# The largest magnitude of v, spread over the partitions by a diagonal matmul on TensorE instead of by an operation on GpSimd

## The chip, the cores and the metric

The kernel runs on one core of a Trainium2 chip. The metric is the device time of one execution in microseconds (us), as the median of several; lower is better. The core has five engines with a queue of instructions each, worked off in order: TensorE (PE in the profile; PEld is its loading of weights), VectorE (DVE), ScalarE (ACT), GpSimd (POOL) and SyncE (SP), which here issues the transfers.

## The reference

Attention with a threshold for 8 batches of 8 heads, 576 positions and 64 columns, then a gated two-layer network over all 4608 tokens:

```python
scores = scale * np.matmul(q, k.transpose(0, 1, 3, 2))
thresh = np.max(scores, axis=-1, keepdims=True) - tau
scores = np.where(scores >= thresh, scores, -1000000000.0)
scores = scores - np.max(scores, axis=-1, keepdims=True)
attn = np.exp(scores)
attn = attn / (np.sum(attn, axis=-1, keepdims=True) + 1e-09)
attn_out = np.matmul(attn, v)
# x: the heads side by side, 4608 x 512; w_in 512 x 2048, w_out 2048 x 512
h = x @ w_in
out = (h * (1.0 / (1.0 + np.exp(-h)))) @ w_out
```

Inputs of attention are float32; the weights come as float64 and are decoded on the chip.

## The kernel before

**Numbers in two halves.** Nearly all products are made with 16-bit operands that are split in a rounded part and the rest (hi and lo), three matmuls for one product. To split v, w_in and w_out into float16 they are first scaled by a power of two that belongs to the largest magnitude. For v this is done anew for each batch: `vmax` (L233) takes the largest magnitude of the four head pairs on each partition, and `vscale` calls `pow2_scales`, which reduces these four (`v_one`, L110), makes the largest over all 128 partitions known to every partition (`v_all`, L113), clamps it (`v_cl`, L116) and takes the two powers of two from its exponent (L120 to L131). `split_v` (L270 on ACT, L271 on DVE) then makes `v16`, hi and lo, which the product with the weights of attention reads. `pow2_scales` is also called for w_in and w_out, but with bounds that are already the same on all partitions, so without the step across them.

**Tiles.** Attention goes by visits of a pair of heads, and in a visit by tiles of 128 queries: batch 0 in two rounds of visits, batches 1 to 7 with nine tiles in each of four visits, 300 slots in all. A tile's work: scores on PE (L406) in one of two PSUM tiles; the maximum on DVE (L416); the exponential on ACT (L426) into one of four buffers `w`; the threshold and the sum on DVE (L435), a reciprocal (L443), the scaling on ACT (L448); then POOL rounds the weights to float16 and makes the rest (`hl`, L459, L462, L465) in one of three buffers, and a transposing DMA puts them into `wT`. Three tiles behind a visit's last, PE multiplies with v (L490), and ACT and DVE split the result to `x16` (L508, L509). POOL also makes the low half of k (`klo`, L320) and, early on, helps to decode the weights (L173, L199).

**Experts.** When all four pairs of a range of tokens are there, its 32 units are put in a list: 16 of `h` (12 matmuls each, L524, then a tanh on ACT, L532, and DVE, L533 and L547, into the buffers g, `gbuf`) and 16 quarters of `o` (12 matmuls each, L562). They are interleaved with the tiles of the next ranges at a rate that spreads them. After the last tile only units are left.

**PSUM.** Unit outputs take banks in turn, by `bank`: two while the weights' sums are taken, three later. A turn is given out in the order of the program's text; the instruction that writes the bank has to wait for the readers of the bank's tenant before.

**Order.** The program is written slot by slot (a slot is a tile), and each step has its slot: `vmax` of pair p of batch b 34 - 9p slots before the batch's first slot u, `vscale` at u - 2, `split_v` at u + 9p + 4, and for batch 0 at slots 0, 1 and 26. A scheduler then orders each engine's queue by readiness on its own timeline, with priorities, so that steps with nothing to wait for come well before their slot. What depends on a buffer or a bank stays behind the step that frees it.

Of the kernel before, what the change touches and what calls it, by code (L numbers as in the profile page):

```python
# [10 lines left out]
BF16 = mybir.dt.bfloat16  # L11
# [8 lines left out]
P = 128  # L20
# [8 lines left out]
GB = 17  # buffers of g: a group of 16 and one ahead  # L29
WSPARE = 2  # raw weights lie this far ahead of the split ones, which take their place  # L30
LOAD = 5  # tiles that the loads of q and k run ahead
AV_LAG = 3  # tiles from a visit's last to its product with v
EARLY = 36  # tiles in which ACT still rounds the weights of attention for GpSimd
GAP, GAP1 = 12, 1  # free slots before batch 0's second visits and before batch 1
V_SLOT = 26  # batch 0's values are split from here on
RATES = (1.3, 0.8)  # units of the experts per slot while batch 0's two groups are there
RATE = 0.95
# weights: first chunk, slots of the decoding and of the splitting, priority
# [3 lines left out]
# a visit of two heads: its tiles of 128 queries (4: the last 64 of both heads) for the  # L42
# first and the second head, and the query ranges that it completes
# [8 lines left out]
def attention_moe(  # L52
# [21 lines left out]
    # three banks in turn; the last one is for the sums of the weights while they come in  # L74
# [7 lines left out]
    # ---------------------------------------------------------------- constants  # L82
    tau_sb = const.tile([P, 1], F32, name="tau_sb")
    nc.sync.dma_start(out=tau_sb, in_=tau)
    # 1/8 where the threshold can be met (tau >= 0), else 0: all scores equal, all kept
# [9 lines left out]
    # stacks of (hi; lo) rows of q, with 64 zero columns for the shared tile  # L95
# [9 lines left out]
    def pow2_scales(mx, name, across=True):  # L105
        """From mx [P, n] (bounds >= 0, per partition or, without across, the same on all):
        s = 2^(13-e) and 1/s for the largest's exponent e."""
# [3 lines left out]
        if across:  # L111
            allp = const.tile([P, 1], F32, name=f"{name}_all", tag=f"{k}_all")
            nc.gpsimd.partition_all_reduce(allp, one, P, bass.bass_isa.ReduceOp.max)  # L113
            one = allp
# [21 lines left out]
    # ---------------------------------------------------------------- weights  # L136
# [29 lines left out]
    def decode_weights(i):  # L166
        """float64 words to float32: the sign, 8 bits of the exponent (2^-112 on the top word
        read as float32 takes the exponent's bias down), 23 of the fraction."""
# [15 lines left out]
        # sums of the magnitudes over the rows of four chunks, four columns at a time: they  # L184
        # bound h (w_in), w_out
# [33 lines left out]
    # ---------------------------------------------------------------- values  # L219
# [56 lines left out]
    # ---------------------------------------------------------------- q and k  # L276
# [12 lines left out]
    def qcol(h, i):  # L289
        """Column of query tile i in the stack (even: 0..3, last, zeros; odd: zeros, last,  # L290
        2, 3, 0, 1)."""
        return i * P if h % 2 == 0 else (0, 384, 512, 128, 256)[(i + 1) % 5]
# [30 lines left out]
    # the first visits work in float32 throughout: the tensor engine has time for them  # L323
# [53 lines left out]
    # ---------------------------------------------------------------- scores  # L377
    # a tile: (visit, [(head, query tile, first row, rows)])
# [98 lines left out]
    # ---------------------------------------------------------------- attn @ v  # L477
    x16 = {}

    def av(v, p, c0, n):  # L480
        """w @ v of the pair's two heads, side by side in the columns of the array: (w hi + w lo) @
        v hi + w hi @ v lo."""
        b = visits[v][0]
        vt = v16[b, p]
# [296 lines left out]
```

## Time and profile before

| | |
|---|---|
| timed runs, median of 3 | 1358.73 us (1357.87 to 1359.26) |
| profiled execution, first to last instruction | 1360.4 us |
| PE busy | 1183.7 us, 87% |
| DVE busy | 1002.8 us, 74% |
| ACT busy | 817.5 us, 60% |
| POOL busy | 789.9 us, 58% |
| mean granted clock of TensorE | 0.95 |

The profile is of one execution beside the timed ones; its span is the only time of it that is shown, 1.7 us above their median. A busy share is a mean over the whole span; the profile also gives it in 40 slices and in any stretch that is asked for. A row of a timeline reads: start, duration, engine, line, operation, output and inputs with their shapes, and in brackets how long the engine was idle before it and what released it; "issue" there means that nothing in the profile released it. A row of stretches gives for each engine the busy time and, in parentheses, the number of instructions, then the granted clock, the share of the DMA engines and GB/s.

### The profile page before, as it was taken

How to read it: one execution, taken by the hardware profiler on the slowest of the kernel's cores; microseconds unless marked ns; L12 is line 12 of the kernel's file. 1: busy time of each engine (PE TensorE's matmuls, PEld its weight loads, DVE VectorE, ACT ScalarE, POOL GpSimd, SP SyncE). 2: the span in 40 equal slices, each digit the busy share in tenths (PEclk: the TensorE clock that was granted, in tenths of full speed). 3: DMA queues.
4: the chain of work that ended last, by engine and by line, in shares of the span. 5: the costliest groups of instructions: out<-in, count | busy, mean ns of one | idle time of the engine just before them, and what ended most of it. 6: DMA issues, size and time to landing. Idle time of an engine off the chain costs nothing.

```text
span 1360.4 us, 26858 instructions
## 1 busy us (share of the span) xinstructions
PE 1183.7 (87%) x9392; PEld 899.9 (66%) x9392; DVE 1002.8 (74%) x2619; ACT 817.5 (60%) x1493; POOL 789.9 (58%) x964
## 2 busy tenths in 40 slices
PE   3774787898599979898899969899799999999998
PEld 2453555666477757676677757677577777777777
DVE  4987997897598967968497856869478787872421
ACT  3776775675476756656375745757367666662432
POOL 2647984787478656754476646556467666661000
PEclk9887888999799999999899979999799999999999
DMA  6454955778467656664475556565466565543000
GB/s 226 140 185 125 197 129 94 146 139 170 88 133 155 122 106 129 131 128 86 99 132 124 118 96 136 101 127 121 82 122 116 115 129 115 106 88 53 6 19 18
DMA packets 363479, 158.15 MB, mean 116 GB/s; under 512 B 329552, under 2 KB 338256, under 8 KB 363344
## 3 DMA queue, kind: packets, MB, share of 16 engines
q1 hardware_dynamic: 363344, 156.43, 55.5%
q8 instruction: 74, 1.21, 0.4%
q14 instruction: 61, 0.50, 0.1%
HBM read 66.72 MB, written 9.44 MB: 56 GB/s over the span
## 4 chain that ended last, share of the span: by engine, by line
DVE 35%; PE 34%; issue 13%; ACT 6%; POOL 6%; DMA 5%; SPq 2%; POOLq 0%; ACTq 0%; DVEq 0%
PE o L562 15%; PE h L524 8%; DVE w L435 8%; DVE sm L416 6%; DVE gbuf L547 6%; PE s L406 5%; PE a L490 5%; DVE qstack L310 3%; DVE th L533 3%; DMA vraw<-in_vL 2%; DMA wT<-hl 2%; ACT w L426 2%; POOL hl L459 2%; POOL hl L462 2%; ACT w L448 2%
## 5 line engine op out<-in xcount | busy, mean ns | idle before, releaser
L524 PE MATMUL h<-x,wst 128*128 128x288 f16 (+2 forms) x3072 | 422.3, 290 | 22.6 <-DVE th L533 19.1
L562 PE MATMUL o<-gbuf,wst 128*128 128x288 f16 (+2 forms) x3072 | 419.4, 293 | 22.4 <-DVE gbuf L547 16.1
L562 PEld LDWEIGHTS <-wst 128*128 128x128 f16 x3072 | 296.4, 100 | 117.1 <-issue 27.1
L459 POOL TENSOR_SCALAR hl<-w 128x576 f16<-128x576 f32 x264 | 187.3, 710 | 317.9 <-ACT w L448 69.1
L524 PEld LDWEIGHTS <-wst 128*128 128x128 f16 x3072 | 290.7, 99 | 119.2 <-issue 37.5
L462 POOL TENSOR_TENSOR hl<-w,hl 128x512 f16<-128x512 f32 x272 | 332.0, 1220 | 28.0 <-issue 13.9
L426 ACT ACTIVATE w<-s,sm 128x576 f32<-128x576 f32 x288 | 211.0, 736 | 204.5 <-POOL hl L465 135.4
L435 DVE SCALAR_TENSOR_TENSOR w<-s,sm,w 128x576 f32<-128x576 f32 x288 | 232.6, 810 | 110.4 <-ACT w L426 108.7
L448 ACT ACTIVATE w<-w,sm 128x576 f32<-128x576 f32 x288 | 218.2, 770 | 86.5 <-DVE sm L443 81.6
L416 DVE TENSOR_REDUCE sm<-s 128x1 f32<-128x576 f32 x288 | 215.1, 748 | 44.4 <-PE s L406 42.3
L406 PE MATMUL s<-khi,qstack 128*128 128x288 f32 x608 | 160.4, 346 | 70.0 <-DVE w L435 36.9
L547 DVE SCALAR_TENSOR_TENSOR gbuf<-th,gbuf 128x288 f16<-128x288 f32 (+2 forms) x256 | 167.3, 656 | 20.9 <-ACT gbuf L541 20.2
L406 PEld LDWEIGHTS s<-khi,qstack 128*128 128x128 f32 x608 | 98.5, 198 | 98.8 <-issue 71.4
L490 PE MATMUL a<-wT,v 128*64 128x288 f16 (+1 forms) x1680 | 142.4, 294 | 16.1 <-DMA wT<-hl 15.0
L532 ACT ACTIVATE th<-h,msc 128x288 f32<-128x288 f32 (+2 forms) x256 | 126.3, 495 | 49.5 <-DVE gbuf L547 30.0
L541 ACT ACTIVATE gbuf<-th 128x288 f16<-128x288 f32 (+2 forms) x252 | 109.9, 438 | 44.5 <-DVE th L533 43.9
L406 PE MATMUL s<-klo,qstack 128*128 128x288 f32 x608 | 134.2, 304 | 0.0
L533 DVE SCALAR_TENSOR_TENSOR th<-th,h 128x288 f32<-128x288 f32 (+2 forms) x256 | 113.2, 444 | 27.6 <-ACT th L532 25.4
L490 PEld LDWEIGHTS <-v 128*64 128x64 f16 x1680 | 91.3, 110 | 56.7 <-issue 41.9
L465 POOL TENSOR_TENSOR hl<-w,hl 128x64 f16<-128x64 f32 x272 | 115.3, 424 | 0.0
L406 PEld LDWEIGHTS s<-klo,qstack 128*128 128x128 f32 x608 | 102.2, 197 | 0.0
L320 POOL TENSOR_TENSOR klo<-kraw,khi 128x576 fp32r<-128x576 f32 x64 | 95.6, 1493 | 1.4 <-ACT khi L318 1.3
(82 smaller groups left out, 868.8 us busy)
## 6 DMA issues: line engine op xcount, KB each, us to landing
qraw<-in_qT SPq DMA_DIRECT2D x128, 144.0 KB, 3.0
kraw<-in_kT SPq DMA_DIRECT2D x128, 144.0 KB, 3.0
vraw<-in_vL SPq DMA_DIRECT2D x32, 320.0 KB, 3.5
wraw<-in_w_out SPq DMA_DIRECT2D x16, 512.0 KB, 4.0
out_t<-ot SPq DMA_DIRECT2D x56, 144.0 KB, 2.0
wT<-hl SPq DMA_TRANSPOSE x304, 3.3
gbuf<-in_w_in SPq DMA_DIRECT2D x8, 512.0 KB, 5.1
wraw<-in_w_in SPq DMA_DIRECT2D x8, 512.0 KB, 4.9
```

What stands on the lines that cost most here:

```text
L406: nc.tensor.matmul(s_ps[:, j, :HALF], lhs, kk[:, j * HALF : (j + 1) * HALF], start=(n == 0), stop=(n == len(seq) - 1),)
L416: nc.vector.tensor_reduce(out=negm, in_=s_ps[:, :, :HALF], op=ALU.max, axis=AX.XY, negate=True)
L426: nc.scalar.activation(wtile[t].rearrange("p (j c) -> p j c", j=2), sps[t][:, :, :HALF], AF.Exp, bias=small[t][:, 0:1],)
L435: nc.vector.scalar_tensor_tensor(out=w3, in0=s_ps[:, :, :HALF], scalar=sm[:, 1:2], in1=w3, op0=ALU.is_ge, op1=ALU.mult, accum_out=sm[:, 2:3],)
L448: nc.scalar.activation(w, w, AF.Copy, scale=r)
L459: nc.gpsimd.tensor_scalar(out=fl[:, 0:S], in0=w, scalar1=1.0, scalar2=1.0, op0=ALU.mult, op1=ALU.mult)
L462: nc.gpsimd.tensor_tensor(out=fl[:, 640:1152], in0=w[:, 0:512], in1=fl[:, 0:512], op=ALU.subtract)
L490: nc.tensor.matmul(a_ps[odd * D : (odd + 1) * D, :n], vt[:, lo_v, odd, kv, :], wT[v, b * H + 2 * p + odd][:, kw, c0 - base : c0 - base + n ...
L524: nc.tensor.matmul(ph[:, :n], wi(c, f, lo_w), x16[b, lo_x][:, c, c0 : c0 + n], start=(k == 0), stop=(k == 11),)
L533: nc.vector.scalar_tensor_tensor(out=th[:, :n], in0=th[:, :n], scalar=1.0, in1=ph[:, :n], op0=ALU.add, op1=ALU.mult,)
L547: nc.vector.scalar_tensor_tensor(out=g[:, 1, :n], in0=th[:, :n], scalar=2.0**-14, in1=g[:, 0, :n], op0=ALU.mult, op1=ALU.subtract,)
L562: nc.tensor.matmul(ps[:, :n], wo(f, d, lo_w), g[:, lo_g, :n], start=(f == 0 and k == 0), stop=(f == NF - 1 and k == 2),)
```

## The change

In `pow2_scales` the branch `across` is replaced. ACT multiplies the rows of an identity matrix (float32, there since the start) with the partition's own largest magnitude, which gives a diagonal matrix in bfloat16. One matmul with a matrix of ones puts the whole diagonal onto every partition, in a PSUM bank taken by `bank`. A DVE reduction takes the maximum over those 128 values. The bfloat16 rounding can move a value up to the next power of two, no further. Nothing else of the code differs but the comments, which are gone in the changed file; its lines from there on have numbers higher by five.

```diff
         if across:
-            allp = const.tile([P, 1], F32, name=f"{name}_all", tag=f"{k}_all")
-            nc.gpsimd.partition_all_reduce(allp, one, P, bass.bass_isa.ReduceOp.max)
-            one = allp
+            diag = const.tile([P, P], BF16, name=f"{name}_diag", tag="diag")
+            nc.scalar.activation(diag, ident, AF.Copy, scale=one)
+            allp = bank([P, P], f"{name}_ps")
+            nc.tensor.matmul(allp, ones, diag, start=True, stop=True)
+            one = const.tile([P, 1], F32, name=f"{name}_all", tag=f"{k}_all")
+            nc.vector.tensor_reduce(out=one, in_=allp, op=ALU.max, axis=AX.X)
```

The scheduler moves much with it. The numbers behind the names below are those of the buffers, and differ between the two programs for the same tile; the number after `w_` is the tile's.

The queue of POOL at tiles 82 to 84, where batch 3's reduction stood before; "ISA" rows without operands are calls that carry no work on a tile:

```order
L459 TENSOR_SCALAR hl_3649<-w_83_3586 128x576
L113 ISA
L113 ISA v_all<-v_one 128x1
L462 ISA
L462 TENSOR_TENSOR hl_3649<-w_83_3586,hl_3649 128x512
L465 TENSOR_TENSOR hl_3649<-w_83_3586,hl_3649 128x64
```

The same place of the change:

```order
L464 TENSOR_SCALAR hl_3661<-w_83_3594 128x576
L464 TENSOR_SCALAR hl_3698<-w_84_3651 128x576
L467 TENSOR_TENSOR hl_3661<-w_83_3594,hl_3661 128x512
L470 TENSOR_TENSOR hl_3661<-w_83_3594,hl_3661 128x64
L467 TENSOR_TENSOR hl_3698<-w_84_3651,hl_3698 128x512
```

The three calls are gone, and the first halves of tiles 83 and 84 come one behind the other.

The queue of DVE at the same tiles, with the reduction on each partition and the clamping, before:

```order
L110 TENSOR_REDUCE v_one<-vmx_3760 128x1
L251 TENSOR_TENSOR msc_5630<-v_sc,i_w_sc 128x1
L252 TENSOR_SCALAR msc_5630<-msc_5630 128x1
L261 SCALAR_TENSOR_TENSOR msc_5630<-msc_5630,o_w_sc 128x1
L416 TENSOR_REDUCE sm_3675<-s_3642 128x1
L435 SCALAR_TENSOR_TENSOR w_84_3639,sm_3638<-s_3589,sm_3638,w_84_3639 128x576
L116 TENSOR_SCALAR v_cl<-v_all 128x1
L419 TENSOR_SCALAR sm_3675<-sm_3675,ntau 128x1
```

In the change `v_one` stands at the same tile, but what follows from it stands 299 rows further down, at tile 125:

```order
L315 SCALAR_TENSOR_TENSOR qstack_85<-qraw_26_5989,gate,qstack_85 64x576
L119 TENSOR_REDUCE v_all<-v_ps 128x1
L424 TENSOR_SCALAR sm_6013<-sm_6013,ntau 128x1
L440 SCALAR_TENSOR_TENSOR w_125_5974,sm_5973<-s_5895,sm_5973,w_125_5974 128x576
L121 TENSOR_SCALAR v_cl<-v_all 128x1
```

Before, the clamping followed `v_one` by six rows, and batch 3's first split of v came 122 rows behind it; now the split comes 14 rows behind `v_all`.

The queue of PE in the change, there and at batch 1 (`v_ps` is the bank with the spread diagonal, `o` and `h` are the experts' banks):

```order
L411 MATMUL s_5977<-klo_5780,qstack_87 128x288 x2
L567 LDWEIGHTS wst
L567 MATMUL o_288_0_5579<-gbuf,wst 128x288
...
L117 LDWEIGHTS ones
L117 MATMUL v_ps<-v_diag,ones 128x128
L567 LDWEIGHTS wst
L567 MATMUL o_288_0_5579<-gbuf,wst 128x288
```

```order
L117 LDWEIGHTS ones
L117 MATMUL v_ps<-v_diag,ones 128x128
L529 LDWEIGHTS wst
L529 MATMUL h_256_1_2375<-x_0_1_452,wst 128x320
L529 LDWEIGHTS wst
L529 MATMUL h_256_1_2375<-x_0_0_451,wst 128x320
L411 MATMUL s_2505<-khi_2412,qstack_85 128x288 x2
L411 MATMUL s_2505<-klo_2414,qstack_85 128x288 x2
```

The matmul is new in PE's queue, between the quarters of an expert's output; six matmuls stand between the scores and it at batch 3, and 216 expert matmuls between it and that batch's first product with v. At batch 1 that number is 26.

## The prediction

> **What bounds the kernel now.** I read the page's busy shares first, then the slices, then the instructions of the line that goes away, then one of its eight places engine by engine, and last the table by stretches.
>
> ```profile
> PE 1183.7 (87%) x9392; PEld 899.9 (66%) x9392; DVE 1002.8 (74%) x2619; ACT 817.5 (60%) x1493; POOL 789.9 (58%) x964
> PE   3774787898599979898899969899799999999998
> ```
>
> The first row says TensorE, 87% busy, and GpSimd (POOL) far from full. The slices (34 us each) say something else: from the middle on TensorE is at 9, with single dips that return about every 155 us, once per batch. So the question is what stops it there.
>
> ```profile
> L113 POOLq MODIFY_POOL_CONFIG  x16: 4/9/13, 11.6 to 951.7; - x16
> L113 POOL PARTITION_ALL_REDUCE v_all<-v_one x8: 377/378/379, 19.1 to 957.3; - x8
>   issue: 43.9, 7
>   DVE v_cl L116: 35.3, 8
> ```
>
> The all-reduce over the partitions is listed with 378 ns, eight times, 3 us in all. But POOL stood idle 43.9 us ahead of seven of them with nothing to wait for, and VectorE (DVE) waited 35.3 us for the eight results. Here is the one of batch 5, by the timelines of POOL, DVE, ACT and PE:
>
> ```profile
> 637.34 0.67 POOL L459 TENSOR_SCALAR hl<-w 128x576 f16<-128x576 f32 x1
> 643.85 0.38 POOL L113 PARTITION_ALL_REDUCE v_all<-v_one  x1 [5.84 <-issue]
> 651.19 0.67 POOL L459 TENSOR_SCALAR hl<-w 128x576 f16<-128x576 f32 x1 [6.96 <-issue]
> ...
> 644.26 0.15 DVE L116 TENSOR_SCALAR v_cl<-v_all 128x1 f32<-128x1 f32 x1 [5.78 <-POOL v_all L113]
> 653.29 0.74 ACT L426 ACTIVATE w<-s,sm 128x576 f32<-128x576 f32 x1 [13.28 <-POOL hl L465]
> 646.05 3.16 PE L562 MATMUL o<-gbuf,wst 128*128 128x288 f16 x13 [4.90 <-DVE gbuf L547]
> 655.04 0.82 PE L406 MATMUL s<-khi,qstack 128*128 128x288 f32 x2 [4.55 <-DVE sm L443]
> ```
>
> POOL stands for 5.84 + 0.38 + 6.96 = 13.2 us, the second gap being in front of an ordinary instruction. Two stalls of TensorE follow. First DVE holds its in-order queue at `v_cl`, behind it the last step of g (L547), for which PE waits 4.90 us. Then ACT's next exponential needs a softmax buffer that POOL has not read yet (13.28 us), DVE waits for ACT, and PE 4.55 us for DVE.
>
> In a sentence of its own: the Trainium skill ("GPSIMD Engine Reference", Instruction dispatch) has the first call of a freshly loaded GpSimd routine pay a load of about 6 us that no instruction shows. The gap in front agrees; the equal one behind is not in that rule, and by one load each POOL would stand 8 x 6 = 48 us where the trace shows 13 us each.
>
> What it costs, by stretches (us and instructions of PE, PEld, DVE, ACT, POOL, then the granted clock):
>
> ```profile
> 20.00:40.00 20.00, 9.90 (x33) 6.82 (x34) 15.06 (x32) 11.07 (x21) 10.31 (x11) 0.71 0.38 114
> 40.00:100.00 60.00, 46.24 (x270) 30.12 (x270) 55.53 (x144) 46.36 (x90) 34.77 (x33) 0.90 0.54 168
> 100.00:120.00 20.00, 9.19 (x57) 6.11 (x54) 11.80 (x31) 9.27 (x16) 10.24 (x11) 0.76 0.37 98
> 120.00:200.00 80.00, 57.88 (x397) 41.77 (x395) 79.32 (x175) 59.26 (x107) 72.87 (x75) 0.83 0.73 165
> 220.00:240.00 20.00, 15.83 (x107) 12.55 (x108) 9.93 (x33) 7.78 (x12) 12.38 (x18) 0.83 0.59 104
> 240.00:340.00 100.00, 89.09 (x703) 65.25 (x700) 85.20 (x224) 67.53 (x117) 76.05 (x94) 0.98 0.77 150
> 340.00:360.00 20.00, 8.24 (x48) 7.14 (x49) 6.35 (x26) 5.62 (x9) 7.45 (x12) 0.57 0.35 58
> 360.00:480.00 120.00, 108.34 (x896) 83.07 (x896) 112.39 (x287) 87.00 (x160) 90.27 (x109) 0.99 0.71 136
> 480.00:500.00 20.00, 15.92 (x110) 11.98 (x109) 11.39 (x37) 8.82 (x16) 6.74 (x11) 0.91 0.27 55
> 500.00:640.00 140.00, 130.94 (x1097) 100.95 (x1098) 112.37 (x299) 91.75 (x170) 89.81 (x114) 1.00 0.65 129
> 640.00:660.00 20.00, 10.55 (x52) 7.24 (x50) 8.22 (x29) 4.06 (x8) 8.19 (x12) 0.74 0.30 65
> 660.00:790.00 130.00, 125.81 (x1072) 97.96 (x1071) 104.89 (x275) 86.22 (x159) 83.74 (x104) 1.00 0.62 124
> 790.00:815.00 25.00, 13.90 (x89) 10.42 (x89) 11.09 (x36) 8.18 (x14) 10.74 (x15) 0.73 0.38 65
> 815.00:950.00 135.00, 126.80 (x1072) 97.83 (x1070) 107.26 (x281) 86.71 (x161) 81.77 (x104) 1.00 0.61 122
> 950.00:975.00 25.00, 15.73 (x89) 11.27 (x88) 10.25 (x38) 8.80 (x14) 11.32 (x17) 0.73 0.46 80
> 975.00:1240.00 265.00, 261.75 (x2221) 202.54 (x2219) 206.95 (x552) 171.34 (x318) 170.21 (x214) 1.00 0.58 110
> 1240.00:1360.00 120.00, 116.62 (x976) 92.66 (x973) 29.86 (x66) 36.59 (x78) 0.00 (x0) 1.00 0.06 18
> ```
>
> The short stretches hold the reduces of batches 1 to 7 (batch 0's is at 19 us), the long ones lie between. From 360 us on the long ones run at 0.99 to 1.00 of the clock with PE 90 to 99% busy; the short ones lose both time and clock. Before 240 us DVE is the full engine (93 and 99%), and its holes are what counts.
>
> **The change, part by part.** *Removed, batches 3 to 7.* In a short stretch I count the matmuls and divide by the rate of the long stretch behind it; the rest of the time is lost. 340: 48 matmuls at 896/120 = 7.47 per us are 6.4 us, lost 13.6. 480: 110 at 7.84, lost 6.0. 640: 52 at 8.25, lost 13.7. 790: 89 at 7.94, lost 13.8. 950: 89 at 8.38, lost 14.4. Sum 61.5 us. Idle time of PE alone is 45.7 us there; the other 16 are matmuls at the lower clock, which goes with the stall. Both come back if POOL keeps working, since PE has a full queue in the long stretches and runs 120 us of pure experts at the end: 1240 to 1360 holds 976 matmuls, 0.123 us each, that only wait for their turn.
>
> By the Trainium skill ("TensorE: Matmul & The Clock Gate", The HAM clock gate) the clock halves after an idle window of about 3.4 us; the trace agrees (0.57 to 0.91 in the stretches where PE stood 4 us and longer at a time, 0.98 and more between). Stalls that stay shorter would cost themselves alone; the sum doesn't change by it.
>
> *Removed, batches 0 to 2.* Here I count DVE's holes against its share in the next long stretch. Batch 2, 220 to 240: 0.85 x 20 - 9.93 = 7 us. Batch 1, 100 to 120: 0.99 x 20 - 11.80 = 8 us. Batch 0:
>
> ```profile
> 19.49 0.15 DVE L116 TENSOR_SCALAR v_cl<-v_all 128x1 f32<-128x1 f32 x1 [6.98 <-POOL v_all L113]
> ```
>
> 6.98 us, and 0.93 x 20 - 15.06 = 3.5 from 20 to 40 us, while POOL cannot decode weights; I take 8 of the 10.5, since the first loads are still landing. Sum 23 us; the ends are 8 (half of DVE's holes are filled by other waits, the first 8 don't shift) and 26.
>
> *Added.* Per batch one ACT copy of 128x128, one weight load and matmul of 128x128, one DVE reduction from PSUM. The nearest rows:
>
> ```profile
> L362 ACT ACTIVATE wT<-tl 128x128 f32<-128x128 f32 x16 | 4.4, 277 | 0.0
> L196 DVE TENSOR_REDUCE wmx<-wps x8: 273/280/291, 46.2 to 178.6; 128x1 f32<-128x128 f32 x8
> L191 PE MATMUL wps<-wst,ones 128*128 128x128 bf16 x128 | 13.9, 244 | 10.8 <-DVE wst L180 10.5 <-DVE sm L439 0.3
> ```
>
> 0.28, 0.28 and 0.24 us. ACT and DVE have 10% or more to spare from 360 us on; PE pays 8 x 0.24 = 2 us.
>
> *Moved.* The order shows that the matmul takes a PSUM bank in turn, so it comes when the program's text comes to it, some 30 tiles after `v_one` and the diagonal copy. PE therefore finds the diagonal ready, and no wait for ACT is added; the matmul stands 2 to 19 expert matmuls behind the scores that DVE reads just before, so DVE waits 0.2 to 2.3 us for it, inside its spare time. But the scale now lies 14 rows ahead of the first split of v. From batch 3 on PE has 216 expert matmuls, 216 x 0.123 = 27 us, between the diagonal matmul and the first product with v, ample. In batch 1 it has 26 matmuls (3.2 us) and three groups of scores, against some 18 DVE rows and two splits; I take 3 us of wait there, between 0 and the longest stall of PE that the trace has:
>
> ```profile
> 115.58 0.85 PE L406 MATMUL s<-khi,qstack 128*128 128x288 f32 x2 [10.57 <-DVE w L435]
> ```
>
> *Sum.* Against the profiled span, 1360.4 - 61.5 - 23 + 2 + 3 = 1281 us. The median of the timed runs is 1.7 us under that span, so **1279 us** is the forecast.
>
> **Rivals.** (1) *Only the first half of each stall goes.* The gap behind the reduce carries the name of no instruction; were it something else (a buffer, a transfer), only DVE's direct wait would vanish. In batch 5 that is 4.90 of the 9.45 us that PE idled, 52%; 0.52 x 84.5 = 44 us gained, and with the 5 us added 1320 us. Against it are the first ordinary POOL instructions behind the reduces of batches 3 and 7, which have the same gap, with nothing to wait for, while the page's releasers elsewhere are named:
>
> ```profile
> 349.07 1.14 POOL L462 TENSOR_TENSOR hl<-w,hl 128x512 f16<-128x512 f32 x1 [6.78 <-issue]
> ...
> 964.73 0.67 POOL L459 TENSOR_SCALAR hl<-w 128x576 f16<-128x576 f32 x1 [7.03 <-issue]
> ```
>
> (2) *The early gain doesn't arrive.* Until 240 us the order of decoding, splitting and scores is changed most, and DVE's holes there may be filled by loads; without the 23 us it is 1302 us. For it: the transfers are 0.38 to 0.73 busy there. Against: DVE's 93 and 99% just after the holes.
>
> (3) *Slower.* The late scale makes the split of v late, and the product with v, in PE's in-order queue, holds the experts behind it. It decides from the point where the chain from the diagonal matmul over DVE's reduction and six small steps to the two splits outlasts the 27 us by 84.5/8 = 10.6 us, which happens to be the longest stall above. At 13.2 us per batch, POOL's standstill put on PE, the sum is 1360.4 - 84.5 + 8 x 13.2 - 1.7 = 1380 us. Against it: the steps behind the matmul are those of `v_cl`, 0.15 us each.
>
> (4) *The reduce stays*, or the queues fall into an order that loses as much elsewhere: no change. POOL's rows hold no such instruction any more.
>
> **How the numbers follow.** Forecast 0.72; (1) 0.10; (2) 0.08; (3) 0.04; (4) 0.02; and 0.04 that yet more goes, below 1262, because the idle time in the stretches from 240 to 480 (10.9 + 11.7 us) is partly the aftermath of the stalls. The range is 1262 (three quarters of those 22.6 us gone as well) to 1312 (no early gain, and 1 us of new waiting per batch on top): it leaves out (1), (3), (4) and the lower tail, 0.20. A change of 0.2% (2.7 us) is what the measurement can tell. Faster 0.94, same 0.02, slower 0.04.
>
> **What would show it.** Right: no instruction of that line on POOL and no 6 us gaps in its queue; the granted clock at 0.98 or more in every 20 us stretch from about 300 us on; PE's busy time a little lower than 1183.7 us and its idle time near 110 us instead of 1360.4 - 1183.7 = 177; the end of attention (1240 us before) some 80 us earlier, and the pure experts behind it still about 120 us. Wrong: dips that stay once per batch, now in front of the products with v (rival 3) or of the scores with POOL as the cause (rival 1); or a start whose first 240 us are as long as before (rival 2).

## The result, and the profile after

The changed kernel takes **1283.62 us** (median of 4 runs, 1280.87 to 1284.8) against 1358.99 us for the kernel before (median of 4, 1357.87 to 1360.19). The ratio is **0.9433, 95% interval 0.9413 to 0.9453**: 75 us or 5.7% faster. The forecast was 1279 us in a range from 1262 to 1312. On another chip the same program took 1281.1 us beside 1362.58, ratio 0.9394 (0.9369 to 0.942). Among the runs below, one execution of chain_twice (2916.86 us) and one of the kernel before (2337.64 us) took about twice as long, for a reason the record doesn't show; the ratios are taken without them.

The page of the changed kernel, busy times first, then two of its rows of slices (32 us each here):

```profile
span 1282.6 us, 26842 instructions
PE 1164.2 (91%) x9400; PEld 891.7 (70%) x9400; DVE 1001.3 (78%) x2627; ACT 819.3 (64%) x1501; POOL 794.6 (62%) x956
PE   5675778799699989999999999999899999999998
PEclk8987899899999989999999999999999999999999
```

The work of DVE, ACT and POOL is what it was, within 5 us each. PE is busy 19.5 us less (1183.7 before) with eight matmuls more, so the same matmuls ran at a higher clock, and it is idle 1282.6 - 1164.2 = 118 us instead of 177. The dips once per batch are gone from the second half of the row PE, but for one 8.

The table by stretches (us and instructions of PE, PEld, DVE, ACT, POOL, then the clock, the DMA share and GB/s). The short stretches up to 760 us lie about where batches 3 to 6 now come by the step (their `v_one` is at 315, 470, 616 and 758 us, 15 to 33 us earlier than before):

```profile
100.00:160.00 60.00, 41.71 (x291) 30.55 (x292) 59.64 (x124) 43.27 (x81) 54.64 (x58) 0.83 0.71 171
160.00:200.00 40.00, 28.59 (x210) 19.28 (x209) 38.98 (x89) 26.98 (x44) 30.20 (x32) 0.96 0.61 113
...
300.00:320.00 20.00, 17.84 (x144) 13.35 (x143) 14.86 (x37) 11.37 (x19) 12.56 (x16) 1.00 0.78 164
...
455.00:475.00 20.00, 15.67 (x131) 12.46 (x130) 15.96 (x41) 9.99 (x16) 12.54 (x15) 0.94 0.56 141
475.00:600.00 125.00, 121.16 (x1008) 93.54 (x1007) 101.02 (x269) 83.28 (x156) 82.40 (x102) 0.98 0.63 122
600.00:620.00 20.00, 18.06 (x152) 14.19 (x150) 16.66 (x48) 10.26 (x17) 12.76 (x15) 1.00 0.65 148
620.00:740.00 120.00, 117.29 (x993) 90.87 (x992) 96.71 (x268) 82.04 (x154) 78.62 (x98) 1.00 0.61 121
740.00:760.00 20.00, 18.79 (x160) 14.68 (x158) 15.26 (x41) 11.00 (x19) 15.59 (x18) 1.00 0.71 161
...
1027.00:1165.00 138.00, 136.16 (x1165) 106.19 (x1163) 104.55 (x283) 87.47 (x161) 87.68 (x110) 1.00 0.56 104
1165.00:1282.00 117.00, 114.23 (x956) 90.74 (x954) 30.01 (x66) 36.37 (x77) 0.00 (x0) 1.00 0.05 16
```

At batch 5's step 152 matmuls now run in 20 us, where the stand's 20 us had 52, and at batch 6's 160; the clock is 1.00 in both. The start is still DVE's (99 and 97% busy from 100 to 200 us), and the pure experts at the end still take 117 us, behind an attention that ends 75 us sooner.

The groups of the chain that was added, with the mean of one in ns and the idle time before it:

```profile
L115 ACT ACTIVATE v_diag<-ident,v_one 128x128 bf16<-128x128 f32 x8 | 3.2, 395 | 0.0
L119 DVE TENSOR_REDUCE v_all<-v_ps 128x1 f32<-128x128 f32 x8 | 2.2, 281 | 0.0
L117 PE MATMUL v_ps<-v_diag,ones 128*128 128x128 bf16 x8 | 1.8, 220 | 0.0
```

None of the three made its engine wait. And of the waits of ACT, this one has halved; the first row is from the kernel before, the second from the changed one (us in total, times, the longest):

```profile
ACT w L426 <- POOL hl L465: 135.4, 54, 14.4
```

```profile
ACT w L431 <- POOL hl L470: 74.8, 47, 5.6
```

The next table places the gains in time, by when the n-th of the 6144 expert matmuls starts. Its head has the times of the kernel before for the 768th, 1536th, 2304th, 3072nd, 3840th and last. The stands of batches 3 and 4 lie between the first two of these times, those of batches 5, 6 and 7 one each in the next three gaps. The rows are the us by which a kernel is ahead (behind, with a minus). Each is one execution: diag_again is the changed kernel once more, and differs from it by up to 7 us; that of pool_spread was the longest of its six. The experiments follow below.

| kernel | 333 | 523 | 681 | 835 | 995 | 1356 |
|---|---|---|---|---|---|---|
| changed | 18.0 | 36.9 | 52.0 | 64.9 | 78.6 | 77.4 |
| diag_again | 18.9 | 43.4 | 57.5 | 70.4 | 85.7 | 84.6 |
| early_only | 21.6 | 18.5 | 18.2 | 18.2 | 21.7 | 14.4 |
| late_only | -2.6 | 20.2 | 35.6 | 48.0 | 62.2 | 60.6 |
| idle_reduce | -7.5 | 2.7 | 1.3 | 2.2 | 8.5 | 7.8 |
| idle_pair | -10.5 | -7.2 | -6.6 | -15.4 | -19.5 | -26.5 |
| pool_spread | 11.7 | 20.1 | 32.0 | 35.3 | 40.9 | 35.3 |
| tile_spread | 20.6 | 38.2 | 49.9 | 53.8 | 63.7 | 53.0 |
| piece_late | 19.1 | 33.9 | 45.1 | 53.6 | 63.0 | 53.9 |

The changed kernel gains 18 us up to 333 us, 19 us over the stands of batches 3 and 4 together, 13 to 15 us over each of the next three, and nothing behind.

### The profile page after: what moved, and what is told of

It is laid out like the page before. It is cut to its first block, busy times and chain, and to the rows that moved or that the text cites. A ratio compares the mean times of both kernels' runs of the same rounds, so it can differ in the third digit from the quotient of the medians.

```text
span 1282.6 us, 26842 instructions
## 1 busy us (share of the span) xinstructions
PE 1164.2 (91%) x9400; PEld 891.7 (70%) x9400; DVE 1001.3 (78%) x2627; ACT 819.3 (64%) x1501; POOL 794.6 (62%) x956
## 4 chain that ended last, share of the span: by engine, by line
PE 45%; DVE 26%; issue 8%; POOL 8%; DMA 7%; ACT 5%; SPq 1%; POOLq 0%; ACTq 0%; DVEq 0%
PE o L567 18%; PE h L529 14%; PE s L411 7%; PE a L495 6%; DVE w L440 5%; DVE sm L421 4%; DVE gbuf L552 4%; DMA wT<-hl 3%; POOL hl L467 3%; DVE qstack L315 2%; DMA vraw<-in_vL 2%; POOL hl L464 2%; DVE th L538 2%; POOL hl L470 2%; DVE wst L185 1%
## 5 line engine op out<-in xcount | busy, mean ns | idle before, releaser
L529 PE MATMUL h<-x,wst 128*128 128x288 f16 (+2 forms) x3072 | 417.2, 289 | 18.0 <-DVE th L538 16.3
L567 PE MATMUL o<-gbuf,wst 128*128 128x288 f16 (+2 forms) x3072 | 403.2, 287 | 8.2 <-DVE wst L211 5.8
L529 PEld LDWEIGHTS <-wst 128*128 128x128 f16 x3072 | 290.5, 99 | 111.8 <-issue 31.2
L567 PEld LDWEIGHTS <-wst 128*128 128x128 f16 x3072 | 289.5, 98 | 95.4 <-DVE wst L211 9.2
L467 POOL TENSOR_TENSOR hl<-w,hl 128x512 f16<-128x512 f32 x272 | 338.3, 1244 | 12.4
L552 DVE SCALAR_TENSOR_TENSOR gbuf<-th,gbuf 128x288 f16<-128x288 f32 (+2 forms) x256 | 158.6, 622 | 22.8 <-ACT gbuf L546 22.0
L495 PE MATMUL a<-wT,v 128*64 128x288 f16 (+1 forms) x1680 | 147.9, 302 | 8.4 <-DMA wT<-hl 6.8
L495 PEld LDWEIGHTS <-v 128*64 128x64 f16 x1680 | 94.7, 114 | 50.2 <-issue 39.5
L470 POOL TENSOR_TENSOR hl<-w,hl 128x64 f16<-128x64 f32 x272 | 122.0, 449 | 0.0
```

What stands on the lines that cost most here:

```text
L467: nc.gpsimd.tensor_tensor(out=fl[:, 640:1152], in0=w[:, 0:512], in1=fl[:, 0:512], op=ALU.subtract)
L470: nc.gpsimd.tensor_tensor(out=fl[:, 576:640], in0=w[:, 512:576], in1=fl[:, 512:576], op=ALU.subtract)
L495: nc.tensor.matmul(a_ps[odd * D : (odd + 1) * D, :n], vt[:, lo_v, odd, kv, :], wT[v, b * H + 2 * p + odd][:, kw, c0 - base : c0 - base + n ...
L529: nc.tensor.matmul(ph[:, :n], wi(c, f, lo_w), x16[b, lo_x][:, c, c0 : c0 + n], start=(k == 0), stop=(k == 11),)
L552: nc.vector.scalar_tensor_tensor(out=g[:, 1, :n], in0=th[:, :n], scalar=2.0**-14, in1=g[:, 0, :n], op0=ALU.mult, op1=ALU.subtract,)
L567: nc.tensor.matmul(ps[:, :n], wo(f, d, lo_w), g[:, lo_g, :n], start=(f == 0 and k == 0), stop=(f == NF - 1 and k == 2),)
```

## The experiments

All diffs are against the changed kernel; ratios are to the kernel before, on the same chip. The theory: GpSimd stands still for 13.2 us per reduction, and that, not DVE's wait for the result, is what TensorE lost.

### The reduction kept, with nobody waiting for it (idle_reduce)

```diff
         if across:
+            unused = const.tile([P, 1], F32, name=f"{name}_un", tag=f"{k}_un")
+            nc.gpsimd.partition_all_reduce(unused, one, P, bass.bass_isa.ReduceOp.max)
             diag = const.tile([P, P], BF16, name=f"{name}_diag", tag="diag")
```

> The diagonal matmul everywhere, and beside it GpSimd's all-reduce as before, into a tile that nobody reads; no engine waits for its result. Theory (POOL stands for 13 us at each, 6 in front and 7 behind, and this alone stops the softmax, while DVE's direct wait is the other half): half of the gain is lost, 1283.6 + 36 = 1320 us (1303 to 1335), PE idle in front of scores but no longer in front of the experts' second half. Rival 1 (the gap behind the reduction belongs to something else, only DVE's direct wait costs): no change from 1283.6 us (1280 to 1290). Rival 2 (DVE's direct wait was covered, POOL alone costs): 1350 us or more.

Measured: 1354.2 us, ratio 0.996 (0.9938 to 0.9981). With DVE free of its wait, 72 to 77 us of the gain are gone (0.996 against 0.9433 and 0.9394). The half that was expected to remain did not; the time is that of the second rival, 1350 us or more. Its timeline at batches 4 and 5:

```profile
513.44 0.38 POOL L115 PARTITION_ALL_REDUCE v_un<-v_one  x1 [6.02 <-issue]
520.87 0.67 POOL L466 TENSOR_SCALAR hl<-w 128x576 f16<-128x576 f32 x1 [7.05 <-issue]
523.08 0.74 ACT L433 ACTIVATE w<-s,sm 128x576 f32<-128x576 f32 x1 [7.09 <-POOL hl L472]
524.83 0.51 PE L413 MATMUL s<-khi,qstack 128*128 128x288 f32 x2 [2.45 <-DVE w L442]
...
662.31 0.38 POOL L115 PARTITION_ALL_REDUCE v_un<-v_one  x1 [6.31 <-issue]
669.62 1.14 POOL L469 TENSOR_TENSOR hl<-w,hl 128x512 f16<-128x512 f32 x1 [6.93 <-issue]
671.06 0.74 ACT L433 ACTIVATE w<-s,sm 128x576 f32<-128x576 f32 x1 [10.70 <-POOL hl L472]
672.81 0.82 PE L413 MATMUL s<-khi,qstack 128*128 128x288 f32 x2 [9.60 <-DVE w L442]
```

In batch 5 PE waits 9.60 us in one go, where it had waited 4.90 and 4.55. The first wait is gone, and the second is as long as the two were together, which fits one cause for both, POOL at a stand. Batch 4 shows the other side: there the stand met a moment at which ACT lost only 7.09 us, and PE then waits 2.45.

### Two such reductions (idle_pair)

```diff
+            unused = const.tile([P, 1], F32, name=f"{name}_un", tag=f"{k}_un")
+            nc.gpsimd.partition_all_reduce(unused, one, P, bass.bass_isa.ReduceOp.max)
+            unused = const.tile([P, 1], F32, name=f"{name}_uo", tag=f"{k}_uo")
+            nc.gpsimd.partition_all_reduce(unused, one, P, bass.bass_isa.ReduceOp.max)
```

> As the run with the unread all-reduce, with two of them per batch. In batches 0 to 4 they stand back to back in POOL's queue, in batches 5 to 7 the scheduler puts one tile's three rounding instructions between them. Theory (the gaps are GpSimd exchanging its code, paid when the kind of instruction changes): back to back the second costs 0.4 to 0.8 us more and POOL stands 13.6 to 14 us; where they are apart each has its own gaps, two times 13 us; the whole is 10 to 35 us slower than with one. Rival (the gaps are the reduction's own time, which the 378 ns don't show): POOL stands 19 to 26 us at a pair back to back too, and the whole is 30 to 60 us slower than with one.

Measured: 1387.82 us, ratio 1.0211 (1.0164 to 1.0257), 33.6 us above the single one. POOL's timeline in batch 4, where the two stand back to back, and in batch 5, where ordinary instructions came between them:

```profile
514.30 0.38 POOL L115 PARTITION_ALL_REDUCE v_un<-v_one  x1 [5.83 <-issue]
514.60 0.42 POOL L117 PARTITION_ALL_REDUCE v_uo<-v_one  x1
522.24 1.14 POOL L471 TENSOR_TENSOR hl<-w,hl 128x512 f16<-128x512 f32 x1 [7.22 <-issue]
...
670.24 0.38 POOL L115 PARTITION_ALL_REDUCE v_un<-v_one  x1 [5.87 <-issue]
677.70 1.14 POOL L471 TENSOR_TENSOR hl<-w,hl 128x512 f16<-128x512 f32 x1 [7.09 <-issue]
...
685.14 0.38 POOL L117 PARTITION_ALL_REDUCE v_uo<-v_one  x1 [6.03 <-issue]
692.89 0.67 POOL L468 TENSOR_SCALAR hl<-w 128x576 f16<-128x576 f32 x1 [7.38 <-issue]
```

Back to back the second costs 0.30 us. Apart, each has both gaps. So the gaps belong to the change from ordinary instructions to this one and back, not to the reduction. In the table of gains the pair lies 8 to 10 us behind the single one at 523 and 681 us, and 34 us at the end: most of the loss comes with batches 5 to 7, where the two are split.

### Only the first three batches, only the last five (early_only, late_only)

```diff
-            diag = const.tile([P, P], BF16, name=f"{name}_diag", tag="diag")
+            if name in ("v0", "v1", "v2"):
+                diag = const.tile([P, P], BF16, name=f"{name}_diag", tag="diag")
...
+            else:
+                allp = const.tile([P, 1], F32, name=f"{name}_all", tag=f"{k}_all")
+                nc.gpsimd.partition_all_reduce(allp, one, P, bass.bass_isa.ReduceOp.max)
+                one = allp
```

The diff is early_only's; late_only has `not in` for `in`.

> The diagonal matmul for batches 0 to 2 alone, GpSimd's all-reduce for batches 3 to 7. Theory (each reduction has its own stall, and the stalls add up): only the gain of the start, 18 us by the shift of the first expert matmuls of batch 2 between the two traces, so 1359 - 18 = 1341 us (1335 to 1347), with five dips of PE as before. Rival (the gain comes from another order that the scheduler finds, not from the stalls): most of the 75 us stays, 1285 to 1310 us.

> GpSimd's all-reduce for batches 0 to 2, the diagonal matmul for batches 3 to 7. Theory: the gain of the PE-bound part, 60 us, so 1359 - 60 = 1299 us (1293 to 1306), and together with the run that has the other batches it gives the whole 75 us within 5. Rival (the scheduler's order): not additive, near 1283 or near 1359 us.

Measured: early_only 1353.36 us, ratio 0.9949 (0.9924 to 0.9973); late_only 1304.72 us, ratio 0.9599 (0.9545 to 0.9653). The late part came as expected. The early part alone is 7.6 us in the medians instead of the 18 expected, outside the 1335 to 1347 us given. Its traced execution is 14.4 us ahead at the end, but it took 1347.45 us, the lowest of its ten runs (up to 1355.9): a trace is one execution, and here not a typical one. The two gains, 0.5 and 4.0%, sum to 4.5%, where both together give 5.7 and 6.1%. They are worth more together than apart; why is open.

### The new chain twice, and in another bank (chain_twice, own_bank, with diag_again beside them)

```diff
             nc.tensor.matmul(allp, ones, diag, start=True, stop=True)
+            first = const.tile([P, 1], F32, name=f"{name}_first", tag=f"{k}_first")
+            nc.vector.tensor_reduce(out=first, in_=allp, op=ALU.max, axis=AX.X)
+            one = first
+            diag = const.tile([P, P], BF16, name=f"{name}_diag", tag="diag")
+            nc.scalar.activation(diag, ident, AF.Copy, scale=one)
+            allp = bank([P, P], f"{name}_ps")
+            nc.tensor.matmul(allp, ones, diag, start=True, stop=True)
```

```diff
-            allp = bank([P, P], f"{name}_ps")
+            allp = ps_a.tile([P, 512], F32, tag="a", name=f"{name}_ps")[:, 0:P]
```

> The changed kernel as it is, to stand beside the other runs of this call on one chip: 0.943 of the time before, as measured first (0.9413 to 0.9453).

> The new chain (diagonal copy on ACT, matmul in a bank of the turn, reduction on DVE) done twice per batch, the second after the first. Theory (each piece costs 0.2 to 0.4 us and only PE's 0.2 us is on the path): 8 x 0.22 = 2 us more than the changed kernel, at most 6 us with DVE's and ACT's part in the DVE-bound start, so 0.944 to 0.948 of before. Rival (each pass through three in-order queues and a bank costs some us that are now hidden in the 4.6 us by which the forecast was too low): 20 us or more, 0.957 and up.

> The spread diagonal goes to the bank of the product with v instead of a bank of the turn. The order shows the matmul of batch 0 some 30 PE rows earlier, and in the other batches between the products with v, still at the end of the batch before; so its place changes little. Theory (the late place is harmless, PE has 27 us of experts behind it): same time as the changed kernel within 5 us. Rival (the late scale and its bank's turn cost something each batch): 10 us faster than the changed kernel; or, if holding the bank of the products is what hurts, slower by as much.

Measured: diag_again 1281.1 us, ratio 0.9394 (0.9369 to 0.942); chain_twice 1275.81, ratio 0.9358 (0.9331 to 0.9385); own_bank 1288.79, ratio 0.9448 (0.9424 to 0.9472). A second pass through ACT, PE and DVE in each batch costs nothing that can be measured, neither the 2 to 6 us of the theory nor the 20 of the rival, so the first has no price to speak of either. The spread diagonal in the bank of the product with v, and no longer in the experts' turn, is 0.5% slower, 7 us: taking it out of the turn gains nothing. That holding the other bank costs the 7 us is the rival's reading, and not shown; and as the matmul's place hardly changes, this run doesn't test whether the late place costs.

### One softmax buffer more (five_buffers_idle_reduce, five_buffers_diag)

```diff
-        t = sb.tile([P, 2, 5, D], F32, tag="vraw", name=f"vraw_{b}_{p}", bufs=5)
+        t = sb.tile([P, 2, 5, D], F32, tag="vraw", name=f"vraw_{b}_{p}", bufs=4)
...
-        w = sb.tile([P, S], F32, tag="w32", name=f"w32_{t}", bufs=4)
+        w = sb.tile([P, S], F32, tag="w32", name=f"w32_{t}", bufs=5)
```

The first of the two has the unread reduction as well; the second is its control.

> The unread all-reduce beside the diagonal matmul, with a fifth softmax buffer w (and four instead of five buffers of raw v, to make room). Theory (ACT's next exponential waits 11 to 13 us for a buffer that POOL hasn't read; a fifth one lets one more tile of about 4 us pass): a third of the loss of each batch goes, 5 to 7 batches x 4 us = 20 to 28 us less than the 70 us lost with four buffers, so 1325 to 1335 us at 1359 us of before, ratio 0.975 to 0.983. Rival (the queues behind the scores stop for another reason, such as POOL's own three buffers or k's low half, which POOL makes too): no change from 0.996.

> The changed kernel with the same two numbers of buffers, as a control: no stall is left that a fifth buffer could cover, so 0.943 of before within 0.005 on either side. If it is slower, fewer buffers of raw v cost, and the other run is read against this one.

Measured: with the reduction 1358.34 us, ratio 0.997 (0.9943 to 0.9998), without it 1292.93, ratio 0.9507 (0.9464 to 0.955). The fifth buffer was to carry ACT over part of the stand, for 20 to 28 us. Against the control the stand still costs 0.046 of 1361 us, 63 us where it was 72 to 77, a difference hardly larger than the intervals. The control itself is about 1% slower than the changed kernel; the raw buffer of v that is missing is the likely reason, but no run has it alone. PE's waits in the kernel with the reduction (total, times, longest):

```profile
PE s L413 <- DVE w L442: 38.6, 20, 8.8
PE a L497 <- DMA wT<-hl: 37.8, 10, 12.3
```

and the second of these in idle_reduce, with four buffers (in the control it is 6.3 us in total):

```profile
PE a L497 <- DMA wT<-hl: 7.9, 5, 4.2
```

The scores may start earlier, but what POOL has not rounded (`hl`) isn't transposed either, and PE stands at the product with v instead. The buffers `w` are one of several links behind POOL.

### Ordinary work on GpSimd in place of the stand (pool_spread, tile_spread, piece_late)

```diff
+            scr = const.tile([P, P], F32, name=f"{name}_scr", tag="scr")
+            with tc.high_priority(offset=2000):
+                nc.gpsimd.tensor_tensor(out=scr[:, 0:1], in0=one, in1=one, op=ALU.mult)
+                nc.gpsimd.memset(scr[:, 1:P], 0.0)
+                for _ in range(32):
+                    nc.gpsimd.tensor_tensor(out=scr, in0=scr, in1=ident, op=ALU.mult)
```

> The changed kernel with 34 ordinary GpSimd instructions of no use per batch (products of 128x128 by the identity, about 0.4 us each, 13 us in all, as much of POOL's time as the reduction held), which the scheduler spreads over the queue: one or two between the tiles' instructions, and a row of 15 to 19 of them in batches 4 to 7. Theory (what cost was POOL standing in one piece, longer than the four buffers of the softmax reach; POOL is 62% busy and has the time): at most 15 us slower than the changed kernel, 0.943 to 0.954 of before. Rival (POOL's time as such is short, whatever its distribution): as slow as with the unread all-reduce, 0.99 and up.

Measured: 1316.47 us, ratio 0.9648 (0.9617 to 0.968): 35 us above diag_again, more than the theory gave and less than the rival. The work came to 142.8 us by its rows, more than the 109 us of idle_reduce's eight stands, and was not well spread: 20 of the instructions ran in one piece of 11.21 us in batch 4, and 15 in one of 8.46 us in each of batches 5 to 7. So two cleaner runs followed. In tile_spread one instruction stands behind the rounding of every tile (272 of them); in piece_late pieces stand in batches 3 to 7 alone, behind `v_one`:

```diff
+        scr = const.tile([P, P], F16, name=f"scr_{t}", tag="scr")
+        nc.gpsimd.tensor_tensor(out=scr, in0=ident, in1=fl[:, 0:P], op=ALU.subtract)
```

```diff
+            if name not in ("v0", "v1", "v2"):
+                scr = [const.tile([P, P], F16, name=f"{name}_scr{i}", tag=f"scr{i}") for i in range(3)]
+                with tc.high_priority(offset=20000):
+                    nc.gpsimd.memset(scr[2][:, 1:P], 0.0)
+                    nc.gpsimd.tensor_tensor(out=scr[2][:, 0:1], in0=one, in1=one, op=ALU.mult)
+                    for i in range(28):
+                        nc.gpsimd.tensor_tensor(out=scr[i % 2], in0=ident, in1=scr[2], op=ALU.subtract)
```

> The changed kernel with one useless subtraction of 128x128 on GpSimd behind the rounding of every tile, into a tile that nobody reads: 288 instructions of about 0.46 us, 125 to 135 us of GpSimd time as in the run with 34 per batch, but none of it in a piece. If what costs is that GpSimd stands for many us in one piece, this is nearly free: at most 12 us above the changed kernel, ratio 0.940 to 0.952. If GpSimd's time itself is short wherever it is taken, the same 35 us or more as there: ratio 0.965 or higher. In between, both count, in that proportion.

> The changed kernel with 30 useless ordinary GpSimd instructions in each of batches 3 to 7, placed so that in batches 4 to 7 some 21 to 26 of them stand behind one another (about 10 to 12 us), and the rest and those of batch 3 in ones and twos; no exchange of code. If a piece of ordinary work costs what the standstill of 13.2 us cost (12 us of 13.2 in each late batch), four pieces of 10 to 12 us cost 35 to 45 us, and with the rest about 40 to 50: ratio 0.970 to 0.980. If the exchange of code has a cost of its own beyond the time that GpSimd stands, the pieces cost clearly less, 20 us or under: ratio 0.957 or lower.

Measured: tile_spread 1309.31 us, ratio 0.962 (0.9558 to 0.9681); piece_late 1307.79, ratio 0.9595 (0.9545 to 0.9645). The changed kernel didn't run beside them, so I take its two ratios, 0.9433 and 0.9394, as ends. Their added instructions:

```profile
L474 POOL TENSOR_TENSOR scr<-ident,hl 128x128 f16<-128x128 f32 x272 | 129.1, 475 | 0.1
```

```profile
L120 POOL TENSOR_TENSOR v_scr<-ident,v_scr 128x128 f16<-128x128 f32 x140 | 56.9, 438 | 0.1
```

With the ten other added ones, piece_late's come to 60 us; its long pieces took 8.15 to 10.49 us, not 10 to 12. What a us of GpSimd cost by these runs (the intervals of the ratios add 3 to 8 us to either side of a loss):

| kernel | added GpSimd time | loss, us | loss per us |
|---|---|---|---|
| tile_spread, 0.48 us at a time | 129 | 25 to 31 | 0.20 to 0.24 |
| pool_spread, partly in pieces | 143 | 35 | 0.24 |
| piece_late, pieces of 8 to 10 us and single ones | 60 | 22 to 27 | 0.36 to 0.45 |
| idle_reduce, stands of 13.0 to 14.8 us | 109 | 72 to 77 | 0.66 to 0.71 |

So the time of GpSimd is not free even in crumbs, though it is 62% busy: tile_spread is within 3 us of the changed kernel up to 681 us (batches 3 to 5 among it), then 11, 15 and 24 us behind. In one stand it is three times as dear. piece_late, in batch 5, shows where the difference lies:

```profile
624.02 8.52 POOL L120 TENSOR_TENSOR v_scr<-ident,v_scr 128x128 f16<-128x128 f32 x22
...
625.02 0.50 PE L418 MATMUL s<-khi,qstack 128*128 128x288 f32 x2 [1.39 <-DVE w L447]
...
635.95 0.74 ACT L438 ACTIVATE w<-s,sm 128x576 f32<-128x576 f32 x1 [4.90 <-POOL hl L477]
```

The piece takes ACT 4.90 us, and PE not more than 1.39 us at a time. Here are the stretches around the pieces of batches 4 and 5 in piece_late, and around the stand of batch 5 in idle_reduce:

```profile
470.00:500.00 30.00, 28.38 (x245) 21.51 (x246) 23.11 (x56) 17.30 (x30) 28.27 (x52) 1.00 0.63 135
618.00:648.00 30.00, 28.45 (x253) 22.17 (x252) 23.86 (x60) 17.45 (x31) 27.95 (x50) 1.00 0.56 126
```

```profile
655.00:690.00 35.00, 23.09 (x183) 17.62 (x181) 18.50 (x52) 15.67 (x29) 15.16 (x21) 0.85 0.44 92
```

PE is 95% busy at full clock around a piece of 8.5 us, and 66% at 0.85 around a stand. The softmax buffers and the scores that lie ready cover a stand of some 8 to 10 us, and not one of 13. That is a reading of these places, not a measurement of the point. And length alone doesn't settle it. In the changed kernel POOL once stands for 13.06 us between two visits, though ACT has scaled three tiles for it by 548 us:

```profile
555.28 0.67 POOL L464 TENSOR_SCALAR hl<-w 128x576 f16<-128x576 f32 x1 [13.06 <-issue]
...
557.49 0.74 ACT L431 ACTIVATE w<-s,sm 128x576 f32<-128x576 f32 x1 [5.29 <-POOL hl L470]
```

ACT waits 5.29 us for POOL, but PE is busy all through 540 to 560 us. Why such a stand costs PE nothing there, and one of the same length at a reduction much, is open.

What piece_late loses gathers little by little: in the table of gains it lies 3 us behind the changed kernel at 523 us, then 7, 11, 16 and 24, and no single wait shows it. Some 8 us of it show only behind 995 us, when the last added instruction (940 us) is long done; why is open.

Ordinary work on POOL also has a cost that no wait shows: beside it DVE's instructions get longer. These are DVE's splits of v (ns, shortest/median/longest), in the changed kernel and in piece_late:

```profile
L276 DVE SCALAR_TENSOR_TENSOR v<-vraw,v_sc,v x32: 862/884/2089, 37.2 to 1053.2; 128x640 f16<-128x640 f32 x32
```

```profile
L283 DVE SCALAR_TENSOR_TENSOR v<-vraw,v_sc,v x32: 861/1123/5220, 36.7 to 1076.5; 128x640 f16<-128x640 f32 x32
```

The one of 5.22 us starts at 778.83 us, in batch 6's piece, and ends when POOL has worked without a break from 772.63 to 784.21 us. DVE is busy 1022.3 us in piece_late and pool_spread and 1011.4 in tile_spread, against 1001.3 and 1004.3 in the two traces of the changed kernel and 1009.9 in idle_reduce. How much of each loss this is isn't measured.

At 0.4 us per us piece_late lies between the two expectations. So the rival of its expectation, that the exchange of code (the change of configuration ahead of a reduction and behind it) costs beyond the time for which POOL stands, is not excluded.

## Why the prediction was right, point by point

**The sum held: 1281 us of span forecast, 1282.6 measured.** *Batches 3 to 7.* 61.5 us less 1.25 for PE's matmuls were forecast; the table of gains gives 77.4 - 18.0 = 59.4, and late_only alone 60.6. Counting the matmuls that a short stretch lacks against its neighbour's rate was the right reading, the clock's share included. From the 768th expert matmul to the end, before and after (PE's busy time is the second number):

```profile
333.20:1360.40 1027.20, 938.88 (x7738) 726.32 (x7736) 725.19 (x1933) 598.44 (x1105) 562.62 (x708) 0.97 0.53 104
```

```profile
315.30:1282.60 967.30, 925.14 (x7742) 720.60 (x7740) 718.66 (x1940) 598.02 (x1109) 571.86 (x705) 0.99 0.56 110
```

PE's idle time falls from 88.3 to 42.2 us, by 46.1 where 45.7 were counted, and its busy time by 13.7 where 16 were put down to the clock. That the total agrees to about a us is partly luck: the trace of diag_again, the same program, gives 84.6 - 18.9 = 65.7.

*Batches 0 to 2.* 23 us less 3.75 were forecast, 18.0 us show at 333 us. The net is right; its parts are not, and that its two misses offset each other is luck. The 3 us wait of batch 1's product with v did not come. The waits of these products from 85 to 300 us (total, times, longest):

```profile
PE a L495 <- DMA wT<-hl: 2.9, 3, 1.5
...
PE a L495 <- DVE x L514: 1.3, 1, 1.3
```

So the gross term was about 4 us too large. By its median early_only says less still, 7.6 us: alone, the early part is not worth what the sum gives it, and why it is worth more beside the late part is open.

*Added.* PE's 0.24 us is 0.22, DVE's 0.28 is 0.28, ACT's 0.28 is 0.39: the nearest row, a copy of the same size, was too low; it has no scale, float32 output and another input, and which of these counts isn't shown. It didn't matter, as chain_twice shows. DVE's wait of 0.2 to 2.3 us for the matmul was not there. DVE had less to spare than the 10% named: from 360 to 480 us it was busy 112.39 of 120 us.

*The last step* took 1.7 us off because the profiled execution of before lay that far above the median. That was one execution's luck, not a constant: after the change the median lies 1.0 us above the span, and in the executions on record that have both, the timed value is 1.7 to 3.2 us above the span of the same execution. The step made the forecast worse by 2.7 of its 4.6 us. *The upper end* of the range is 1310 us by its own terms (1279 + 23 + 8), not 1312.

**The reading that failed** is "Two stalls of TensorE follow": the split into a first stall by DVE's `v_cl` and a second by POOL's unread buffer, as if each could go alone. From it rival (1) got its 1320 us for a kernel in which only DVE's wait goes. idle_reduce is that kernel, and takes 1354: PE waits the whole 9.60 us at the second place. The forecast was safe from this, since the change removes both. It would have been wrong by 34 us for a change that only moved the wait.

**The reading of the clock** was too simple as well. The stretch from 480 to 500 us before (0.91) has no wait of PE longer than 3.6 us, the one from 220 to 240 us (0.83) none longer than 3.05, and before 240 us the long stretches too have only 0.83 to 0.90. That the clock's share came back with the stalls holds, as the busy time shows; that shorter stalls cost themselves alone doesn't, as the last of these rows of the changed kernel shows, whose longest wait of PE stands below them:

```profile
320.00:340.00 20.00, 13.75 (x112) 10.65 (x109) 16.29 (x47) 13.67 (x22) 16.21 (x22) 0.91 0.77 146
460.00:480.00 20.00, 15.67 (x128) 11.94 (x127) 14.89 (x38) 8.51 (x15) 7.70 (x9) 0.83 0.52 137
900.00:920.00 20.00, 16.90 (x134) 13.10 (x132) 13.43 (x37) 10.06 (x18) 8.73 (x11) 0.91 0.48 90
```

```profile
PE s L411 <- DVE sm L424: 2.6, 1, 2.6
```

**The rivals.** (1) fell by the result, and by idle_pair: the gap behind the reduction is of the same kind as the one in front. It should have had less than 0.10, for the trace of before names it, in rows that the prediction doesn't use; by line, in the kernel before (ns, shortest/median/longest, first to last start in us):

```profile
L459 POOLq MODIFY_POOL_CONFIG  x8: 82/83/83, 218.3 to 957.7; - x8
...
L462 POOLq MODIFY_POOL_CONFIG  x4: 83/83/83, 342.2 to 800.0; - x4
```

POOL's own queue changes its configuration ahead of the ordinary instruction too: at 957.7 us, and the instruction starts at 964.73, 7.0 us later, as the reduction starts at 957.3 behind its own change at 951.7, 5.6 us later. (2) fell: 18 us were there at 333 us. (3) fell: PE waits for neither the scale nor the splits, and its costliest wait from 340 to 1165 us is for the scores' tiles:

```profile
PE s L411 <- DVE w L440: 11.1, 10, 4.3
```

(4) fell: the instruction is gone, and so is the time.

**What would show it.** No such instruction on POOL: yes. No 6 us gaps in its queue: no, the sign was badly chosen. Gone are the gaps around the changes of configuration; but POOL still is idle for 6 to 13 us about once per visit, as it was before, and PE loses nothing at the longest of these, shown above. Clock of 0.98 in every 20 us stretch from 300 us: not in the three just shown, about the steps of batches 3, 4 and 7. PE's idle time 118 us, not 110. Attention 75 us shorter instead of 80, the pure experts 117 us.

## What to carry to other kernels

A short row can hide a long one: look at the idle time in front of an engine's odd instruction and of the first ordinary one behind it, and at its queue's configuration rows, and charge the sum to the kernel (here 0.38 us shown, 13.2 us taken, about 9 us of time lost each). Where an engine stands, ask who is served by its other work, not who waits for that one result: taking the waiter away gave back 7 us, taking the stand away 75. A spare engine's mean share says little; by these runs it matters more for how long at a time it leaves waiting work undone. But at one place 13.06 us of that cost PE nothing, so the length has to be read together with what the engines behind still have to do.

## What the runs showed of the hardware that was not expected

**The way back costs as much as the way there.** In the rows shown, an isolated reduction came 5.84 to 6.31 us behind the instruction before it, and the next ordinary instruction 6.78 to 7.38 us behind the reduction. Two reductions back to back pay once, with 0.30 us between them. The Trainium skill ("GPSIMD Engine Reference", Instruction dispatch) has about 6 us for the first call of a freshly loaded routine. The trace agrees for the way there, with 5.6 us from the change of configuration to the reduction; what the runs add is that with ordinary instructions in between it is paid each time again, in both directions.

**Stalls and clock go together.** Around PE waits of 9.60 us the granted clock was 0.85, around waits of up to 1.39 us it was 1.00. The Trainium skill ("TensorE: Matmul & The Clock Gate", The HAM clock gate) has the clock halve after an idle window of about 3.4 us. The runs go lower: in the changed kernel's stretch from 900 to 920 us the clock was 0.91 with no wait of PE longer than 2.64 us. How short a wait must be to leave the clock alone isn't shown.

**Reducing across partitions by TensorE is the cheaper way here.** The Trainium skill ("GPSIMD Engine Reference", Engine selection) gives GpSimd for a reduction along partitions; the runs here go against that. In this kernel 0.39 + 0.22 + 0.28 us on three engines with room did it for 128 values, and the kernel is 5.7% faster by it.
